# The order of one DMA queue in a mixture-of-experts loop, and a fourth staging buffer in two slots

## The chip, the core and the metric

The kernel runs on one core of a Trainium2 chip. The time is the device time of one execution in microseconds, the median of three runs. Its engines are PE (TensorE), ACT (ScalarE), DVE (VectorE), POOL (GpSimd) and SP (SyncE), which here only issues DMAs.

## The reference, cut to what matters

Three layers follow each other: an attention over 2 x 8 heads of 768 rows, a mixture of eight experts in which each of 1536 tokens goes to one expert, and a feed-forward layer with a rational function in place of an activation.

```python
for e in range(E):                      # layer 2: N, D, E, F = 1536, 512, 8, 1024
    mask = expert_idx == e
    h = np.maximum(x[mask] @ w1[e], 0.0)
    out[mask] = gate_w[mask, None] * (h @ w2[e])
...
h = x @ w_in                            # layer 3: 512 -> 2048 -> 512
P = a[0] + a[1] * h + a[2] * h2 + a[3] * h3
Q = 1.0 + np.abs(b[0]) * np.abs(h) + np.abs(b[1]) * h2
return (g @ w_out).astype(np.float32)
```

`w_in` and `w_out` arrive as 64-bit floats, and the kernel has to turn them into 32-bit floats by bit operations.

## The kernel before

The tokens are sorted by expert and worked on in 17 **slots** of 128 rows (`NSL`, L1069; loop at L1075). Slot s does the first product of its rows (`gemm1(s)`, into `ph`), transposes the rows of slot s + 1 (`xtr`), does the second product of slot s - 1 (`gemm2(s - 1)`, into `py`) and transposes its own hidden rows (`htr(s)`, into `pht`, then `hhi` and `hlo`). This document counts a slot from its first matmul of `gemm1` (L901) to the next slot's.

Every product is done with operands split in a high and a low part. ACT writes the high part of a weight half (`whi`, L654) and DVE the low part (`wlo`, L657), from four raw buffers `rw[s % 2, part]` of 2 MB each. Neighbouring slots often have the same expert. Then neither the loads of `wload` (L533, with a condition) nor the split of `wsplit` take place; both are decided by a flag in a table that the program computes.

**The conversion jobs.** While the slots run, 26 jobs convert layer 3's weights, two to a slot in slots 1 to 11 (`job_at`, L1072), one to a slot in 12 to 15. Job j takes five steps. `conv_load` (L858) is issued one slot ahead: 512 KB into one of four buffers `cx` or, from job 22 on, into a part of `el`. `conv_a` (L862, ACT) writes the high words' absolute value into a buffer z of 256 KB, which is one of the eight parts of the tile `el`. `conv_c` (L867, POOL) clamps z, `conv_b` (L872, L875 and L878, DVE) shifts and joins the bits, and `conv_s` (L883) stores z to `wf` in the next slot. Jobs up to 17 take z = `el` part j % 6; later ones 4 + j % 3. Jobs 16 and 17 have parts 4 and 5, jobs 18 to 21 the parts 4, 5, 6 and 4. Parts 0 to 3 are the load buffers of jobs 22 to 25. Part 7 is used by no job; layer 3's first weights are loaded into it at L1002 from slot 14 on.

Nothing reorders the instructions: each engine takes them in the order in which the code writes them. On ACT a slot reads: high parts of the next first half, `relu`, `xhi`, the slot's `conv_a`, the scaling of `y` (L937), `hhi` (L919), high parts of the second half. So a `conv_a` that waits holds back `hhi`, without which the next `gemm2` can't begin. On SP a slot reads: the store of the sorted rows of `y` (`ysave`, L949), loads for layer 3, the next jobs' `conv_load`, `x2load` (L957), eight weight loads in two halves (`wload(s + 2, 0)` and `wload(s + 1, 1)`), and last `conv_s` of the slot before. `ysave` and each half of `wload` first read registers from the table.

Of the kernel before, what the change touches and what calls it, by code (L numbers as in the profile page):

```python
# [13 lines left out]
I32 = mybir.dt.int32  # L14
# [45 lines left out]
NX, NM = 22, 26  # L60
# [18 lines left out]
def tile_kernel(ctx, tc, I, out):  # L79
# [13 lines left out]
    el = elp.tile([P, 8, TT], F32, name="el")  # L93
# [429 lines left out]
    def wload(s, part, ks=range(4)):  # L523
        r = rw[s % 2, part]
        src = I["w1"] if part == 0 else I["w2"]
        if s > 1:
            ev = nc.sync.value_load(rg[0:1, 1, s:s + 1], min_val=0, max_val=E - 1)
            fl = nc.sync.value_load(rg[0:1, 3, s:s + 1], min_val=0, max_val=1)
        for k in ks:
            if s < 2:  # L530
                nc.sync.dma_start(out=r[:, k], in_=src[s, :, k])
            else:
                nc.sync.dma_start(out=r[:, k],  # L533
                                  in_=src[bass.ds(ev, 1), :, k].rearrange("o p f -> (o p) f"), cond=fl > 0)
# [81 lines left out]
    def gather(s):  # L616
        xg[s] = gx[s % 3]
        nc.gpsimd.indirect_dma_start(out=xg[s], out_offset=None, in_=xs,
                                     in_offset=bass.IndirectOffsetOnAxis(ap=idx[:, s:s + 1], axis=0))
# [207 lines left out]
    cv = []  # L827
# [4 lines left out]
    def wsplit(s, part, which="hl"):  # L832
        if s == 0:
            split(s, part)
        elif which != "hl":
            e = ENG.Activation if which == "h" else ENG.DVE
            fl = nc.values_load(rg[0:1, 3, s:s + 1], engines=[e], min_val=0, max_val=1)
            with tc.If(fl > 0):
                for k in range(4):
                    if which == "h":  # L840
                        shi(s, 4 * part + k)
                    else:
                        slo(s, 4 * part + k, nc.vector)
        else:
            fl = nc.values_load(rg[0:1, 3, s:s + 1], engines=[ENG.Activation, ENG.DVE], min_val=0, max_val=1)
            with tc.If(fl > 0):  # L846
                split(s, part)
# [4 lines left out]
    def conv_load(j):  # L852
        if cv:
            cvt[j] = cv[0].tile([P, 512, 2], I32, name="cvt")
        else:
            t = el[:, 2 * (j % 2):2 * (j % 2) + 2].rearrange("p a b -> p (a b)") if j >= NX else cx[j % 4]
            cvt[j] = t.bitcast(I32).rearrange("p (a b) -> p a b", b=2)
        nc.sync.dma_start(out=cvt[j].rearrange("p a b -> p (a b)"), in_=I["wio"][j // 2, :, j % 2].bitcast(I32))  # L858

    def conv_a(j):  # L860
        z = el[:, 6 + j % 2 if cv else j % 6 if j < NX - 4 else 4 + j % 3].bitcast(I32)
        nc.scalar.activation(out=z.bitcast(F32), in_=cvt[j].bitcast(F32)[:, :, 1], func=AF.Abs)  # L862
        cvt[j] = (cvt[j], z)

    def conv_c(j, eng):
        z = cvt[j][1].bitcast(F32)
        eng.tensor_scalar(out=z, in0=z, scalar1=CLO, scalar2=CHI, op0=ALU.max, op1=ALU.min)  # L867
# [14 lines left out]
    def conv_s(j):  # L882
        nc.sync.dma_start(out=wf[j // 2, :, j % 2], in_=cvt.pop(j).bitcast(F32))  # L883
# [9 lines left out]
    def gemm1(s):  # L893
        hi, lo = xTm.pop(s)
        ph = [ps_h.tile([P, 512], F32, name=f"ph{n}") for n in range(2)]
        for rl in (False, True):
            kn = [(k, n) for k in range(4) for n in range(2)]
            for k, n in kn:
                w = (wlo if rl else whi)[:, k, 512 * n:512 * n + 512]
                for l in (hi,) if rl else (hi, lo):  # L900
                    nc.tensor.matmul(out=ph[n], lhsT=l[:, k], rhs=w, start=(k == 0 and not rl and l is hi),  # L901
                                     stop=(k == 3 and rl))
        hsb[s] = (hb, ph)

    def relu(s):
        h, ph = hsb[s]
        for n in range(2):
            nc.scalar.activation(out=h[:, 4 * n:4 * n + 4], in_=ph[n].rearrange("p (a b) -> p a b", a=4),
                                 func=AF.Relu)
# [36 lines left out]
    def ysave(s):  # L946
        y = yt.pop(s)
        yv = nc.sync.value_load(rg[0:1, 2, s:s + 1], min_val=0, max_val=(MAXS - 1) * P)
        ins = nc.sync.dma_start(out=ys[bass.ds(yv, P)], in_=y).ins  # L949
        for c, l in xld.items():  # L950
            if s >= c + MAXS - NT + 1:
                tc.declare_no_dep(ins, l, reason=APART)
        ysv[s] = ins

    def x2load(c):
        xid[c] = xa.tile([P, DR], F32, name="x2", bufs=2)
        ins = nc.sync.dma_start(out=xid[c], in_=ys[c * P:(c + 1) * P]).ins  # L957
        for s, l in ysv.items():
            if s >= c + MAXS - NT + 1:
                tc.declare_no_dep(ins, l, reason=APART)  # L960
        xld[c] = ins
# [32 lines left out]
    def fload(c, p):  # L994
        if (c, p) in floaded:
            return
        if (c, p) in ((0, 0), (1, 0)):
            wr[c, p] = el[:, 7]
        else:
            wr[c, p] = ring[(len(floaded) - 2) % len(ring)]  # L1000
        floaded.append((c, p))
        nc.sync.dma_start(out=wr[c, p], in_=wf[c, :, p])  # L1002

    def fsplit(c, p):
        if (c, p) in fdone:
            return
        fdone.append((c, p))
        r = wr[c, p]
        hi, lo = fsp[c % FH][p]
        nc.scalar.activation(out=hi, in_=r, func=AF.Copy)  # L1010
        (nc.gpsimd if cv else nc.vector).tensor_tensor(out=lo, in0=r, in1=hi.bitcast(F32), op=ALU.subtract)  # L1011
# [51 lines left out]
    def regather(s):  # L1063
        nc.gpsimd.indirect_dma_start(out=xg[s], out_offset=None, in_=xs,
                                     in_offset=bass.IndirectOffsetOnAxis(ap=idx[:, s:s + 1], axis=0))
# [3 lines left out]
    NSL = MAXS - 2  # L1069
    cxp = cx_.enter_context(tc.tile_pool(name="cx", bufs=1, reuse_waits="tile"))  # L1070
    cx += [cxp.tile([P, 1024], F32, name=f"cx{i}") for i in range(4)]
    job_at = {s: (2 * s - 2, 2 * s - 1) for s in range(1, NX // 2 + 1)}  # L1072
    for j in range(NX, NM):
        job_at[j - NX // 2 + 1] = (j,)
    for s in range(NSL + 1):  # L1075
        mine = job_at.get(s, ())
        if s == NX // 2 + 1:
            cx_.close()
            xb = ctx.enter_context(tc.tile_pool(name="xb", bufs=1, reuse_waits="tile"))
            x2.append((xb.tile([P, 4, TT], F32R, name="x2h0"), xb.tile([P, 4, TT], F32R, name="x2l0")))  # L1080
        if s and s + 2 < NSL:
            gather(s + 2)
        if s > 1:
            ysave(s - 2)
        if s >= NSL - 2:
            fsplit(s - (NSL - 2), 0)
        if s >= NSL - 3:
            fload(s - (NSL - 3), 0)
        for j in job_at.get(s + 1, ()):
            conv_load(j)  # L1090
        if 0 <= s - (NSL - 6) < 6:
            x2load(s - (NSL - 6))
        if s < NSL:
            gemm1(s)
            if STOP and s == 1:
                moe.close()
                rawr.close()
                return
            if s + 2 < NSL:
                wload(s + 2, 0)  # L1100
            if s + 1 < NSL:
                wload(s + 1, 1)
            for j in job_at.get(s - 1, ()):
                conv_s(j)
            if s + 1 < NSL:
                wsplit(s + 1, 0, "h")
            relu(s)
            if s + 1 < NSL:
                xtr(s + 1)
                wsplit(s + 1, 0, "l")  # L1110
            if s == 0:
                regather(1)
                for i in range(2):
                    nc.gpsimd.tensor_copy(out=gts[:, i:i + 1], in_=xg.pop(i)[:, DM:DM + 1])
            for j in mine:
                conv_a(j)
            for j in mine:
                conv_c(j, nc.gpsimd)
        if s > 0:
            gemm2(s - 1)  # L1120
            if s == NSL - 1:
                wsplit(s, 1, "h")
                htr(s)
            if s == NSL:
                elem_a(0)
                elem_b(0)
                elem_c(0)
            gemm2e(s - 1)
            if s == NSL - 1:
                wsplit(s, 1, "l")  # L1130
                fg1(0)
            if 0 <= s - (NSL - 5) < 4:
                x2prep(s - (NSL - 5))
        if s < NSL - 1:
            htr(s)
            wsplit(s, 1)
        for j in mine:
            for k in range(3):
                conv_b(j, k)
# [102 lines left out]
    for i in range(NI + 2):  # L1242
        j = conv_at.get(i, 0)
# [32 lines left out]
        if i + 1 in conv_at:  # L1276
            conv_a(conv_at[i + 1])
# [100 lines left out]
```

## Time and profile before

| | |
|---|---|
| time, median of 3 runs | 634.88 us (634.71 to 638.09) |
| profiled execution | 635.7 us |
| its span, first to last instruction | 633.9 us |
| PE busy | 578.4 us (91%) |
| DVE, ACT, POOL busy | 478.5, 417.8, 289.3 us |
| mean granted TensorE clock | 0.969 of full speed |

The span has three parts: attention and sorting to about 109 us, the 17 slots to about 344 us, and layer 3. The times of rows are microseconds from the span's start. A slot can be read from PE's rows: two `gemm1` that follow each other begin a slot apart.

### The profile page before, as it was taken

The page shows a single profiled execution, that of the slowest core. Times are in us where ns is not written, and L with a number is a line of the kernel's source. Part 1 is how long each engine was busy: PE and PEld are TensorE (multiplying, and loading weights), DVE is VectorE, ACT ScalarE, POOL GpSimd, SP SyncE. Part 2 cuts the span into 40 slices and gives each one's busy share as a digit, 9 for nine tenths or more (in the row PEclk, how much of TensorE's full clock was granted, in tenths as well). Part 3 has the DMA queues.
Part 4 walks back from the last instruction along what each step waited for, and adds up shares of the span by engine and source line. Part 5 has one row for each costly group of instructions (what it writes and reads, how often), then busy time and mean ns, then how long its engine had stood idle before and what let it go on. Part 6 is the DMA issues. An engine that isn't in the chain of part 4 may idle for free. (4 is left out here: it accounts for less than half of the span.)

```text
span 633.9 us, 10217 instructions
## 1 busy us (share of the span) xinstructions
PE 578.4 (91%) x3112; PEld 468.2 (74%) x3112; DVE 478.5 (75%) x1012; ACT 417.8 (66%) x719; POOL 289.3 (46%) x313
## 2 busy tenths in 40 slices
PE   4888984999999998879999899989999999999994
PEld 4777973688888887668887677777777777888883
DVE  6978877787845893369767777888988867877874
ACT  6987644775535672276765888766767887776672
POOL 7948822537334540454131654424244664432324
PEclk9989985999999999979999999999999999999998
DMA  9999541587669984779873422211114200000101
GB/s 273 321 306 295 169 166 50 165 335 250 232 204 308 397 288 150 229 243 336 323 249 101 134 73 94 67 51 50 51 50 150 77 24 1 34 34 1 51 17 67
DMA packets 37854, 101.65 MB, mean 160 GB/s; under 512 B 5977, under 2 KB 6105, under 8 KB 37794
## 3 DMA queue, kind: packets, MB, share of 16 engines
q1 hardware_dynamic: 35314, 92.81, 44.6%
q0 software_dynamic: 2480, 8.15, 3.6%
q8 instruction: 25, 0.41, 0.3%
q14 instruction: 35, 0.29, 0.1%
HBM read 119.51 MB, written 19.18 MB: 219 GB/s over the span
## 5 line engine op out<-in xcount | busy, mean ns | idle before, releaser
L867 POOL TENSOR_SCALAR el<-el 128x512 f32<-128x512 f32 x32 | 68.2, 2139 | 111.4 <-ACT el L862 111.4
L1051 POOL TENSOR_TENSOR wlo<-el,whi 128x512 fp32r<-128x512 f32 (+1 forms) x33 | 43.1, 1306 | 84.6 <-issue 44.7
L657 DVE TENSOR_TENSOR wlo<-rw,whi 128x1024 fp32r<-128x1024 f32 x62 | 74.6, 1263 | 2.1 <-issue 1.4
L654 ACT ACTIVATE whi<-rw 128x1024 fp32r<-128x1024 f32 x64 | 63.2, 1053 | 9.7 <-POOL wlo L657 4.4
L930 PE MATMUL py<-whi,hhi 128*128 128x512 f32 x136 | 56.1, 412 | 8.6 <-ACTq L846 8.6
L887 PE MATMUL hg<-x2h,whi 128*128 128x512 f32 (+1 forms) x148 | 58.7, 396 | 3.2 <-DVE el L1045 3.2
L888 PE MATMUL hg<-x2h,wlo 128*128 128x512 f32 (+1 forms) x148 | 57.7, 390 | 0.0
L889 PE MATMUL hg<-x2l,whi 128*128 128x512 f32 (+1 forms) x148 | 57.5, 389 | 0.0
L901 PE MATMUL ph<-whi,xhi 128*128 128x512 f32 x136 | 56.4, 415 | 0.7 <-ACT xhi L647 0.7
L1043 DVE SCALAR_TENSOR_TENSOR el<-el,ab,hg 128x512 f32<-128x512 f32 (+1 forms) x49 | 36.0, 735 | 26.5 <-ACT hg L1039 26.1
L901 PE MATMUL ph<-whi,xlo 128*128 128x512 f32 x136 | 55.1, 405 | 0.2 <-issue 0.2
L920 DVE TENSOR_TENSOR hlo<-pht,hhi 128x512 fp32r<-128x512 f32 x34 | 21.8, 682 | 43.8 <-ACT hhi L919 31.3
L930 PE MATMUL py<-whi,hlo 128*128 128x512 f32 x136 | 54.7, 402 | 0.0
L889 PE MATMUL acc<-wlo,whi 128*128 128x512 f32 x130 | 51.7, 398 | 2.0 <-POOL wlo L1011 1.7
L1029 ACT ACTIVATE el<-hg,ab 128x512 f32<-128x512 f32 (+1 forms) x49 | 33.2, 677 | 30.6 <-PE hg L889 30.5
L887 PE MATMUL acc<-whi 128*128 128x512 f32 x130 | 51.3, 395 | 2.1 <-DVE part L1221 1.0
L888 PE MATMUL acc<-whi,wlo 128*128 128x512 f32 x130 | 51.2, 394 | 1.2 <-POOL wlo L1051 1.2
L1031 DVE SCALAR_TENSOR_TENSOR el<-el,ab,hg 128x512 f32<-128x512 f32 (+1 forms) x49 | 35.9, 732 | 18.1 <-ACT el L1030 18.1
L1037 ACT ACTIVATE el<-el 128x512 f32<-128x512 f32 (+1 forms) x49 | 30.6, 624 | 28.5 <-DVE el L1031 28.0
L1033 DVE SCALAR_TENSOR_TENSOR el<-el,ab,hg 128x512 f32<-128x512 f32 (+1 forms) x49 | 36.1, 737 | 1.7
L1030 ACT ACTIVATE el<-hg,ab 128x512 f32<-128x512 f32 (+1 forms) x49 | 37.4, 763 | 0.0
L930 PEld LDWEIGHTS py<-whi,hhi 128*128 128x128 f32 x136 | 26.2, 193 | 14.7 <-ACTq L846 9.1
(354 smaller groups left out, 1557.2 us busy)
## 6 DMA issues: line engine op xcount, KB each, us to landing
rw<-w SPq DMA_DIRECT2D x136, 512.0 KB
cx<-wio SPq DMA_DIRECT2D x22, 512.0 KB
wf<-el SPq DMA_DIRECT2D x32, 256.0 KB
vw<-vp SPq DMA_DIRECT2D x8, 585.0 KB
ys<-y SPq DMA_DIRECT2D x17, 257.0 KB
xg<-wf SPq DMA_DIRECT2D x13, 256.0 KB
xs<-xall SPq DMA_DIRECT2D x12, 257.0 KB
x<-ys SPq DMA_DIRECT2D x12, 257.0 KB
```

Of the source, the lines that this page charges most:

```text
L654: nc.scalar.activation(out=whi[:, i], in_=rw[s % 2, i // 4][:, i % 4], func=AF.Copy)
L657: eng.tensor_tensor(out=wlo[:, i], in0=rw[s % 2, i // 4][:, i % 4], in1=whi[:, i].bitcast(F32), op=ALU.subtract)
L867: eng.tensor_scalar(out=z, in0=z, scalar1=CLO, scalar2=CHI, op0=ALU.max, op1=ALU.min)
L887: nc.tensor.matmul(out=o, lhsT=lh, rhs=rh, start=start, stop=False)
L888: nc.tensor.matmul(out=o, lhsT=ll, rhs=rh, start=False, stop=False)
L889: nc.tensor.matmul(out=o, lhsT=lh, rhs=rl, start=False, stop=stop)
L901: nc.tensor.matmul(out=ph[n], lhsT=l[:, k], rhs=w, start=(k == 0 and not rl and l is hi), stop=(k == 3 and rl))
L930: nc.tensor.matmul(out=py, lhsT=l[:, f], rhs=w, start=(f == 0 and not rl and l is hi), stop=(f == 7 and rl))
L1030: nc.scalar.activation(out=u, in_=h, func=AF.Identity, scale=ab[:, 3:4], bias=ab[:, 2:3])
L1033: nc.vector.scalar_tensor_tensor(out=u, in0=u, scalar=ab[:, 1:2], in1=h, op0=ALU.add, op1=ALU.mult)
L1043: nc.vector.scalar_tensor_tensor(out=u, in0=u, scalar=ab[:, 0:1], in1=h, op0=ALU.add, op1=ALU.mult)
L1051: nc.gpsimd.tensor_tensor(out=lo, in0=g, in1=hi.bitcast(F32), op=ALU.subtract)
```

## The change

On SP the slot's DMAs are put in another order: after `ysave` comes the first half of the weights (`wload(s + 2, 0)`), then `x2load`, the stores `conv_s` of the slot before, the loads `conv_load` of the slot after, and last the second half of the weights (`wload(s + 1, 1)`). And jobs 18 to 21 take the `el` parts 4, 5, 6 and 7 instead of 4, 5, 6 and 4.

```diff
     def conv_a(j):
-        z = el[:, 6 + j % 2 if cv else j % 6 if j < NX - 4 else 4 + j % 3].bitcast(I32)
+        z = el[:, 6 + j % 2 if cv else j % 6 if j < NX - 4 else j - NX + 8 if j < NX else 4 + j % 3].bitcast(I32)
...
-        for j in job_at.get(s + 1, ()):
-            conv_load(j)
-        if 0 <= s - (NSL - 6) < 6:
-            x2load(s - (NSL - 6))
         if s < NSL:
             gemm1(s)
...
             if s + 2 < NSL:
                 wload(s + 2, 0)
+            if s >= NSL - 6:
+                x2load(s - (NSL - 6))
+            for j in job_at.get(s - 1, ()):
+                conv_s(j)
+            for j in job_at.get(s + 1, ()):
+                conv_load(j)
             if s + 1 < NSL:
                 wload(s + 1, 1)
-            for j in job_at.get(s - 1, ()):
-                conv_s(j)
```

The first place is SP's queue in slot 10, before the change: `ys` is the store of sorted rows, `cx0` and `cx1` are the loads of jobs 20 and 21, `rw00` and `rw11` the two halves of the weights (each load stands four times in the queue, here once), and the `wf` row is the stores of jobs 16 and 17.

```order
L949 DMA ys_1758<-y0_1750 128x514
L858 DMA cx0_1769<-wio 128x1024
L858 DMA cx1_1770<-wio 128x1024
L527 TENSOR_LOAD rg_160
...
L533 DMA rw00_68<-w1 128x1024
...
L533 DMA rw11_1740<-w2 128x1024
...
L883 DMA wf_1759<-el_64 128x512 x2
```

The same slot of the same queue after the change:

```order
L949 DMA ys_1758<-y0_1750 128x514
L527 TENSOR_LOAD rg_160
...
L533 DMA rw00_68<-w1 128x1024
...
L883 DMA wf_1759<-el_64 128x512 x2
L858 DMA cx0_1769<-wio 128x1024
L858 DMA cx1_1770<-wio 128x1024
...
L533 DMA rw11_1740<-w2 128x1024
```

The two stores have moved ahead of the two loads and of four weight loads, and the first half of the weights ahead of the two loads.

The second place is ACT's queue in slot 11, before the change, from `xhi` to the first `hhi`; the two L862 rows are `conv_a` of jobs 20 and 21, and the names in brackets are the counters that a row waits for (DMAHW3 to 5 count DMAs).

```order
L647 ACTIVATE xhi_1591<-px__3942 128x512 [waits DVE_49,PE_49]
L862 ACTIVATE el_64<-cx0_1769 128x512 [waits DMAHW4_49]
L838 UNCONDITIONAL_BRANCH
L862 ACTIVATE el_64<-cx1_1770 128x512 [waits DMAHW5_49,DMAHW3_49,DVE_49]
L937 ACTIVATE y0_1750<-py_3969,gts_1382 128x512 [waits PE_49]
```

The same rows after the change:

```order
L647 ACTIVATE xhi_1591<-px__3942 128x512 [waits DVE_49,PE_49]
L862 ACTIVATE el_64<-cx0_1769 128x512 [waits DMAHW2_49]
L862 ACTIVATE el_64<-cx1_1770 128x512 [waits DMAHW3_49]
L838 UNCONDITIONAL_BRANCH
L937 ACTIVATE y0_1750<-py_3969,gts_1382 128x512 [waits PE_49]
```

`conv_a` of job 21 waited for two DMAs and for DVE; now it waits for one DMA, its own load, as that of job 20 did and does.

## Rows read from the trace of the kernel before

**Rows 1.** Stretches: us; busy PE, PEld, DVE, ACT, POOL; PE clock; DMA share; GB/s.

```profile
208.09:220.63 12.54, 12.54 (x64) 10.25 (x62) 9.87 (x14) 8.25 (x14) 5.99 (x5) 1.00 1.03 409
233.15:245.67 12.52, 12.52 (x64) 10.24 (x62) 10.03 (x14) 6.50 (x10) 1.05 (x1) 1.00 0.67 208
245.67:261.37 15.70, 12.80 (x63) 10.31 (x62) 5.83 (x10) 5.00 (x9) 7.71 (x5) 1.00 0.36 103
261.37:281.95 20.58, 14.90 (x68) 11.98 (x66) 7.28 (x12) 9.15 (x14) 4.96 (x4) 0.83 0.77 257
281.95:294.91 12.96, 12.96 (x67) 10.67 (x66) 11.76 (x15) 8.00 (x13) 4.75 (x5) 1.00 1.01 401
294.91:307.89 12.98, 12.98 (x68) 10.69 (x66) 9.20 (x13) 8.16 (x13) 9.15 (x7) 1.00 0.90 291
```

**Rows 2.** PE in time: start, length, line, tiles, idle before and releaser.

```profile
251.38 0.60 PE L645 MATMUL px__3942<-cst,xg 128*128 128x128 f32 x4
254.87 0.50 PE L930 MATMUL py<-whi,hhi 128*128 128x512 f32 x1 [2.90 <-ACTq L846]
...
273.35 0.79 PE L930 MATMUL py<-whi,hhi 128*128 128x512 f32 x1 [5.68 <-ACTq L846]
273.94 0.63 PE L930 MATMUL py<-whi,hlo 128*128 128x512 f32 x1
...
277.23 0.39 PE L930 MATMUL py<-whi,hlo 128*128 128x512 f32 x1
```

**Rows 3.** ACT in time, slots 10 and 11, with rows of slots 8 and 13.

```profile
215.94 1.23 ACT L862 ACTIVATE el<-cx 128x512 f32<-128x512 f32 x2
...
239.85 0.60 ACT L647 ACTIVATE xhi<-px__3745 128x512 fp32r<-128x512 f32 x1
251.90 1.33 ACT L862 ACTIVATE el<-cx 128x512 f32<-128x512 f32 x2 [11.44 <-issue]
...
257.45 0.68 ACT L862 ACTIVATE el<-cx 128x512 f32<-128x512 f32 x1
271.04 0.66 ACT L862 ACTIVATE el<-cx 128x512 f32<-128x512 f32 x1 [12.90 <-issue]
...
293.38 0.69 ACT L862 ACTIVATE el<-el 128x512 f32<-128x512 f32 x1 [4.07 <-DMA wf<-el]
```

**Rows 4.** SP in time: issues of DMAs, how many in a row.

```profile
199.88 1.77 SPq L858 DMA_DIRECT2D cx<-wio  x2
...
234.02 4.75 SPq L533 DMA_DIRECT2D rw<-w  x8
238.82 0.81 SPq L883 DMA_DIRECT2D wf<-el  x2
240.75 0.34 SPq L949 DMA_DIRECT2D ys<-y  x1
241.70 2.13 SPq L858 DMA_DIRECT2D cx<-wio  x2
245.33 4.39 SPq L533 DMA_DIRECT2D rw<-w  x8
249.76 0.81 SPq L883 DMA_DIRECT2D wf<-el  x2
...
266.55 1.59 SPq L883 DMA_DIRECT2D wf<-el  x2
283.74 0.85 SPq L883 DMA_DIRECT2D wf<-el  x2
```

**Rows 5.** DVE in time: the last steps of jobs 15, 16 and 17.

```profile
231.18 0.98 DVE L878 SCALAR_TENSOR_TENSOR el<-cx,el 128x512 int32<-128x512 int32 x1
240.98 0.69 DVE L878 SCALAR_TENSOR_TENSOR el<-cx,el 128x512 int32<-128x512 int32 x1
242.77 0.69 DVE L878 SCALAR_TENSOR_TENSOR el<-cx,el 128x512 int32<-128x512 int32 x1
```

**Rows 6.** A shorter stretch in slot 11, columns as in rows 1.

```profile
247.00:257.00 10.00, 7.10 (x33) 5.60 (x32) 2.46 (x5) 3.87 (x8) 4.32 (x3) 1.00 0.14 53
```

## The prediction, written before the run

> **What bounds the kernel now.** I read the page's busy shares first (PE 91%), then the stretches slot by slot, then PE, ACT, SP and DVE in order of time around the two slots that stick out.
>
> In the slots PE is the bound: slots 8 and 10 take 12.54 and 12.52 us and PE is busy in all of it, and slots 13 and 14, which also transpose rows for layer 3, take 12.96 and 12.98, again full [rows 1]. Slot 11 takes 15.70 and slot 12 takes 20.58 [rows 1]. Slot 12 has the same extra transposes as slot 13, so the two are 15.70 - 12.52 = 3.18 and 20.58 - 12.96 = 7.62 us too long, 10.80 together.
>
> PE shows where: its first `gemm2` matmul stood idle 2.90 us in slot 11 and 5.68 us in slot 12 [rows 2]. These are 8.58 of the 10.80. After the longer gap the clock is down: the matmuls take 0.63 instead of 0.39 us for a while, and slot 12's mean granted clock is 0.83 where the others have 1.00 [rows 1, 2]. That costs about 1.7 us: 277.23 - 273.35 = 3.88 us for nine matmuls that take nine steps of about 0.235 us at full clock, 2.1. The rest is the restart.
>
> The releaser named is a branch in ACT's queue, so I look at ACT. In slot 10 its pair of `conv_a` (jobs 18 and 19) began at 251.90 after 11.44 us of idleness; in slot 11 `conv_a` of job 20 ran at once at 257.45, and that of job 21 only at 271.04, after 12.90 us [rows 3]. "Issue" says that the view sees no releaser among the engines. SP has it: the stores of jobs 16 and 17 were issued at 249.76, and 2.14 us later the pair starts; the stores of jobs 18 and 19 were issued at 266.55, and 4.49 us later job 21 starts [rows 4, 3]. Jobs 18 and 19 write `el` parts 4 and 5, which jobs 16 and 17 left there until they are stored, and job 21 writes part 4, which holds job 18. The stores stand last in SP's slot, behind the loads and eight weight loads. PE waits for `hhi`, which is behind `conv_a` on ACT.
>
> **The buffers.** Job 21 now writes part 7, job 20 part 6 as before. The order of ACT's waits shows for both only their own load. Nothing else holds part 7 in slot 11, since layer 3's load into it comes from slot 14 on. So the 12.90 us wait goes, and slot 12 falls to slot 13's 12.96: **-7.62**. What is late next is the load of the pair. It was issued at 241.70; now it stands behind the two stores and, as worked out below, is issued at about 244, some 9 us before ACT reaches it. ACT reached `xhi` 6.70 us into slot 10 (239.85 - 233.15) [rows 1, 3], so 245.67 + 7.3 = 253.0 in slot 11. The bound on the other side: if another wait kept job 21 at its place, this term is 0.
>
> **The stores.** Jobs 18 and 19 still write parts 4 and 5, so in slot 10 only the order can help. Job 16 is ready for storing at 240.98 + 0.69 = 241.67 and job 17 at 243.46 [rows 5]. Does SP get there? In slot 9 it can't pass before job 15 is done, at 231.18 + 0.98 = 232.16 [rows 5]. Then come one store issue (0.40), two loads (about 0.9), the second half of the weights, `ysave` and the first half. Eight weight loads with one read of registers inside take 4.75 us, and a read takes about 1.5 us (243.83 to 245.33) [rows 4]; four loads are then 1.6 and a half with its read 3.1. `ysave` ends 1.46 us after the stores before it (239.63 to 241.09) [rows 4]. 232.16 + 0.40 + 0.9 + 3.1 + 1.46 + 3.1 = 241.1: in time. With 2.14 us from issue to release, job 19 may start at 243.46 + 2.14 = 245.6 instead of about 252.6 (251.90 and half of 1.33). From there to PE's first matmul it took 254.87 - 252.57 = 2.30 us, so `gemm2` may begin at 247.9; PE itself comes to it at about 251.38 + 0.35 = 251.73 [rows 2]. That is 3.8 us of slack, and the 2.90 us stall goes too: **-3.18**.
>
> The uncertain size is the time from the store's issue to its release. The trace has 2.14, 4.49 and, for a store behind eight weight loads, 283.74 to 293.38 = 9.64 us [rows 3, 4]. By 4.49 job 19 starts at 248.0 and there is still no stall. By 9.64 it starts at 253.1, PE at 255.4, 3.7 us late: 0.5 us worse than now. The store now stands behind four weight loads. But in that stretch they move little: 208 GB/s in slot 10 and 53 GB/s from 247 to 257, against 409 in slot 8 [rows 1, 6], so few of the weight loads there can take place. So I take 2.14, the nearest row, and keep +0.5 as the other end.
>
> The Trainium skill speaks against this (DMA: Bandwidth & Descriptors, section on queues, rings and completion order): on each DMA engine the descriptors are consumed in the order of the ring, so what is put behind 2 MB of weights waits for them. The 9.64 us row agrees. Were those 2 MB moved in slot 10, at slot 8's 409 GB/s they would add 5.1 us, job 19 would start at 250.7 and PE at 253.0; the stall would be 1.3 instead of 2.90 us and the sum 1.3 us smaller.
>
> **What it costs.** No instruction is added: SP issues the same DMAs. Loads of conversions now stand behind the first half and two stores: (2.1 + 0.5) MB at 409 GB/s [rows 1], 6.4 us, in slots where the expert changes. The cover is the distance from issue to use: 199.88 to 215.94 for the jobs of slot 8, 16.1 us [rows 3, 4]. A landing after 6.4 + 2.6 (their own 1.05 MB) + 2.1 = 11 us is in time; once the cover is gone, each further microsecond beyond the 3.8 of slack costs PE one. The second half now waits for the stores, and so for `conv_b`; but before, both halves stood behind `conv_load`, which waits for the same `conv_b` (its buffer `cx` is the one that `conv_b` reads). The weights are needed a slot later, and PE never waited for them in rows 1's full slots. I cost all this at nothing, with 0 to 1 us as its bounds. The first half gets earlier, which gains nothing for the same reason.
>
> **The sum.** 7.62 + 3.18 = 10.80 off the profiled execution's 635.7: 624.9, and a span of 623.1. The median is 0.82 below the profiled execution, so 624.1. I expect the whole saving to reach the end, since layer 3 starts from the last slots and has no work of its own that runs on a clock of its own.
>
> **Rivals.**
> *Only the buffer helps.* Slot 11's stall stays, because SP arrives late or the stores are slow to be released. For it: the order of the queue gives slot 10 a margin of only half a microsecond on SP (241.1 against 241.67), though the slack is 3.8 behind it. Then 634.88 - 7.62 = 627.3, or 627.8 with the 0.5. Chance 0.11.
> *Given back in the next slots.* The two stalls let DVE and the DMAs catch up: over slots 11 to 14 they moved 103 x 15.70 + 257 x 20.58 + 401 x 12.96 + 291 x 12.98, 15.9 MB in 62.2 us, and must do so in 51.4 us: 309 GB/s, under slot 8's 409; DVE has 34.1 us of work in them [rows 1]. So the sums fit, but a second half queued behind 6.4 us of other transfers could stall slot 13 or 14 by as much: 624.1 + 6.4 = 630.5. Chance 0.07.
> *Slower: the conversion loads come late.* Where first halves are moved, `conv_load` lands after them, `conv_a` waits, and the stall of slot 11 shows up in other slots. It decides once a load takes over 16.1 + 3.8 = 19.9 us from issue to landing. With 3.18 us in each of six slots (about the number in which a first half of a new expert is loaded) it costs 19.1: 624.1 + 19.1 = 643. Against it: 11 us by the rates. Chance 0.04.
> *The change does nothing:* job 21 would have to wait for something in part 7. The list of its waits excludes it; I give it no share.
>
> **How the numbers follow.** The forecast has 0.78; its own range is 622.5 to 626.5 (a microsecond of cost, and the spread of the runs, which went up to 3.4 us). With the first rival's 627.3 to 627.8 and a part of the second, 622.0 to 629.0 holds 8 in 10 or a little more. About 0.5%, 3.2 us, is what a measurement can tell from no change here; faster means under 631.7. The forecast and the first rival lie there, and most of the second: 0.78 + 0.11 + 0.03 = 0.92, which I round down to 0.90 for what I haven't thought of; same 0.06; slower 0.04.
>
> **What would show it.** Right: slots 11 and 12 of 12.5 and 13.0 us, no idle time before `gemm2` in either, clock 1.00 in slot 12, the store of job 16 issued at about 242 (9 us into slot 10), `conv_a` of slot 10 starting 10 to 13 us into the slot and that of slot 11 right behind `xhi`. Wrong: a `conv_a` that waits in another slot, a `whi` that waits for `rw`, or stalls at the start of layer 3 that were not there.

## The result, and the profile after

The changed kernel takes 631.71 us (median of 21 runs), the kernel before 637.41 us (21 runs too): 5.70 us less. These medians count every run, while the ratios, here and below, leave out a kernel's slow runs, those over 1.5% above its fastest (5 of these 21, one of the kernel before's 21, 3 of the 6 of e4 below). The ratio is 0.9887, 95% interval 0.9862 to 0.9913: 7.2 us faster (5.5 to 8.8). 10.80 was forecast, and the time is 2.7 us above the predicted range.

The execution that was profiled with this timing took 641.43 us, far above the median, so the rows here are from a second profile of the same kernel (e1_after, span 631.0 us); the first one is called the first profile below. Stretches of that kernel, with the columns of [rows 1]; the rows are slots 0, 1, 10, 11 and 12:

```profile
112.36:123.00 10.64, 10.14 (x36) 7.64 (x37) 7.00 (x7) 5.75 (x9) 6.33 (x4) 0.72 0.22 44
123.00:140.80 17.80, 14.35 (x63) 11.16 (x61) 11.79 (x13) 8.08 (x12) 8.35 (x9) 0.90 0.99 355
...
240.99:253.51 12.52, 12.52 (x64) 10.25 (x62) 10.03 (x14) 7.18 (x11) 2.06 (x4) 1.00 0.56 191
253.51:266.05 12.54, 12.54 (x64) 10.26 (x62) 5.58 (x10) 5.49 (x11) 8.56 (x8) 1.00 0.84 244
266.05:279.02 12.97, 12.97 (x68) 10.69 (x66) 10.40 (x14) 8.14 (x13) 4.67 (x4) 1.00 0.90 321
```

Slots 11 and 12 took 15.70 and 20.58 before [rows 1] and take 12.54 and 12.97 now: 10.77 us less, as forecast. But slot 1 is 17.80 us long, with PE busy for 14.35 of them and a clock of 0.90. The prediction uses no row of slots 0 and 1 of the kernel before; here they are, in the same view:

```profile
109.06:119.71 10.65, 9.60 (x37) 6.99 (x37) 7.00 (x7) 5.77 (x9) 6.19 (x4) 0.80 0.30 70
119.71:132.94 13.23, 13.01 (x62) 10.10 (x61) 12.12 (x13) 7.93 (x12) 9.04 (x7) 1.00 0.96 336
```

Slot 1 has lost 17.80 - 13.23 = 4.57 us. All other slots agree within 0.1 us, and layer 3, from the start of slot 16 to the end, takes 313.07 us before and 313.06 after. From the start of slot 0 to that of slot 16 it is 211.79 us before and 205.55 after, 6.24 less. The first profile agrees with 205.21 us for that stretch, and its slot 1 is long too:

```profile
132.07:149.48 17.41, 14.56 (x62) 11.35 (x61) 11.70 (x13) 8.09 (x12) 8.52 (x9) 0.90 0.97 355
```

PE in order of time, columns as in [rows 2]: first slot 1, then slots 11 and 12.

```profile
132.68 1.09 PE L645 MATMUL px__1981<-cst,xg 128*128 128x128 f32 x4 [3.23 <-DMA xg<-xs,idx]
...
133.99 0.63 PE L930 MATMUL py<-whi,hlo 128*128 128x512 f32 x1
...
259.21 0.60 PE L645 MATMUL px__3942<-cst,xg 128*128 128x128 f32 x4
259.57 0.48 PE L930 MATMUL py<-whi,hhi 128*128 128x512 f32 x1
...
271.75 0.60 PE L645 MATMUL px__4145<-cst,xg 128*128 128x128 f32 x4
272.10 0.48 PE L930 MATMUL py<-whi,hhi 128*128 128x512 f32 x1
```

The first `gemm2` matmul of slots 11 and 12 follows the transposes with no bracket, that is, with no idle time before it: the stalls of 2.90 and 5.68 us [rows 2] are gone. In slot 1 the transposes of `px` wait 3.23 us for a DMA into `xg`, the rows that POOL gathers for slot 2; then matmuls take 0.63 us for a while, as they did in slot 12 before [rows 2].

ACT, answering [rows 3], in slots 10 and 11, then SP, answering [rows 4], in slot 10:

```profile
247.69 0.61 ACT L647 ACTIVATE xhi<-px__3745 128x512 fp32r<-128x512 f32 x1
251.88 0.67 ACT L862 ACTIVATE el<-cx 128x512 f32<-128x512 f32 x1 [3.58 <-DVE el L878]
253.81 0.67 ACT L862 ACTIVATE el<-cx 128x512 f32<-128x512 f32 x1 [1.26 <-DMA wf<-el]
...
260.21 0.61 ACT L647 ACTIVATE xhi<-px__3942 128x512 fp32r<-128x512 f32 x1
260.69 1.24 ACT L862 ACTIVATE el<-cx 128x512 f32<-128x512 f32 x2
```

```profile
247.72 1.47 SPq L533 DMA_DIRECT2D rw<-w  x4
249.56 2.13 SPq L883 DMA_DIRECT2D wf<-el  x2
251.74 0.92 SPq L858 DMA_DIRECT2D cx<-wio  x2
254.22 1.49 SPq L533 DMA_DIRECT2D rw<-w  x4
```

The wait of 11.44 us ahead of slot 10's pair is 3.58 and 1.26, and that of 12.90 us ahead of job 21 is gone: its `conv_a` runs right behind job 20's, 0.48 us after `xhi` started. The stores were issued 8.6 us into slot 10 (predicted 9), and the pair started 10.9 and 12.8 us into it (predicted 245.6 - 233.15 = 12.45 for the second).

### The profile page after: what moved, and what is told of

Same layout as the page of the kernel before. It is cut to its first block, busy times and chain, and to the rows that moved or that the text cites. A ratio compares the mean times of both kernels' runs of the same rounds, so it can differ in the third digit from the quotient of the medians.

```text
span 639.7 us, 10251 instructions
## 1 busy us (share of the span) xinstructions
PE 589.9 (92%) x3112; PEld 478.5 (75%) x3112; DVE 476.4 (74%) x1012; ACT 417.7 (65%) x719; POOL 284.4 (44%) x313
## 5 line engine op out<-in xcount | busy, mean ns | idle before, releaser
L867 POOL TENSOR_SCALAR el<-el 128x512 f32<-128x512 f32 x32 | 65.1, 2042 | 103.5 <-ACT el L862 103.5
L1029 ACT ACTIVATE el<-hg,ab 128x512 f32<-128x512 f32 (+1 forms) x49 | 33.1, 676 | 30.9 <-PE hg L889 30.8
L937 ACT ACTIVATE y<-py,gts 128x512 f32<-128x512 f32 x17 | 11.7, 685 | 45.2 <-PE py L930 40.3
L280 ACT ACTIVATE at<-sm,nm 128x118 f32<-128x118 f32 x96 | 29.7, 381 | 14.5 <-DVE nm L272 14.4
```

## Experiments

The theory from these rows: the stalls went as forecast, and the new order made one of its own in slot 1, by putting the second half of slot 1's weights beside POOL's row gathers. Rivals: the conversion loads do it, not the weights; slot 1's length is a whim of an execution, and the missing gain lies elsewhere. Kernels that ran together share the runs of the kernel before on their chip, 11 each time: e1 to e4 a median of 641.27 us, e5 to e8 of 636.43, e9 to e11 of 636.25.

**e1_after**: the changed kernel again.

> The changed kernel as it is, for a second profile and more times. Theory A (the new order issues the weights of slots 0 and 1 while the row gathers are on their way, so that slot 2's rows come late): slots 11 and 12 of 12.5 and 13.0 us, slot 1 again about 17.4 us with PE idle some 2.6 us before the transposes of slot 2's rows, and 10.8 - 4.2 = 6.6 us under the kernel before. Rival B (slot 1's stall belongs to the one execution that was profiled): slot 1 of 13.2 us and some 10.8 us under the kernel before.

Measured 630.84 us (6 runs), ratio 0.9864 [0.9801, 0.9928]; rows above. POOL's queue in slots 0 and 1 of this kernel, then SP's (start, length, line, idle before and releaser):

```profile
122.17 0.95 POOL L618 DMA_INDIRECT xg<-xs,idx  x1 [0.30 <-issue]
...
133.88 0.57 POOL L1114 COPY gts<-xg 128x1 f32<-128x1 f32 x1 [6.30 <-DMA xg<-xs,idx]
```

```profile
119.71 1.49 SPq L533 DMA_DIRECT2D rw<-w  x4
121.31 0.83 SPq L858 DMA_DIRECT2D cx<-wio  x2
122.23 3.19 SPq L531 DMA_DIRECT2D rw<-w  x4
```

The same two queues in the kernel before:

```profile
119.02 0.95 POOL L618 DMA_INDIRECT xg<-xs,idx  x1 [0.30 <-issue]
```

```profile
117.13 0.81 SPq L858 DMA_DIRECT2D cx<-wio  x2
119.81 2.53 SPq L533 DMA_DIRECT2D rw<-w  x4
122.44 2.27 SPq L531 DMA_DIRECT2D rw<-w  x4
```

POOL issues three gathers there, 1.3 us apart; the middle one (L618) fetches slot 2's rows. It is issued at about the same point of slot 0 in both (119.02 - 109.06 = 9.96 us in, and 122.17 - 112.36 = 9.81). The second half of the weights (L531) comes 13.38 us into slot 0 before and 9.87 after: 3.42 us behind the gather before, 0.06 us behind it now. PE uses the rows 10.5 us after the gather's issue (132.68 - 122.17), and it waited for them; before it used them 7.0 us after the issue (119.02 to 126.00), without a wait. POOL, which copies a column of slot 1's rows (L1114), waits 6.30 us for the third gather too. PE at slot 2's transposes in the kernel before:

```profile
126.00 0.60 PE L645 MATMUL px__1981<-cst,xg 128*128 128x128 f32 x4
```

Why the second half comes so much earlier shows in SP's waits of the kernel before (total us, times, longest):

```profile
SPq L858 <- DMA xs<-xall: 2.7, 1, 2.7
```

The conversion loads stand first in the old slot 0 and wait there for a store into `xs` (L519), with the register reads and both halves of the weights behind them. In the new order the reads and the first half stand ahead of these loads. From the issue of that store to the second half it takes 8.51 us before (113.93 to 122.44) and 5.00 in e1 (117.23 to 122.23).

**e2_buffer_only** and **e3_order_only**: each half of the change alone.

```diff
 # e2_buffer_only: of the change only this
+        z = el[:, 6 + j % 2 if cv else j % 6 if j < NX - 4 else j - NX + 8 if j < NX else 4 + j % 3].bitcast(I32)
 # e3_order_only: the whole change without that line
```

> The old order with the new buffer rule (jobs 18 to 21 in parts 4 to 7). Theory A: slot 12 falls from 20.6 to 13.0 us, slot 11 keeps 15.7, slot 1 keeps 13.2: 7.6 us under the kernel before, and so about as fast as the whole change or 1 us faster. Rival C (the two stalls come from the order, the buffer matters little): 3 us or less under.

> The new order with the old buffer rule (job 21 in part 4, which job 18 holds). Theory A: slot 11 of 12.5 us; in slot 11 job 18 is ready about 5 to 6 us after the slot's start (DVE ends it at about 250.9) and its store lands some 4 us later, about 2 to 3 us after ACT wants the part, which the slack of 3.8 us covers: slot 12 near 13.0, at most 15; slot 1 of 17.4. So 4 to 6.6 us under the kernel before, close to the whole change. Rival C' (without the fourth buffer slot 12's stall stays): slot 12 of 20.6, slot 1 of 17.4, 1 us over the kernel before.

Measured: e2 632.39 us, ratio 0.9899 [0.984, 0.9957]; e3 631.07 us, 0.987 [0.981, 0.993]. Slots 11, 12 and 15 of e2, then slots 1, 11 and 12 of e3:

```profile
247.66:263.35 15.69, 12.79 (x63) 10.30 (x62) 5.83 (x10) 6.15 (x12) 8.52 (x6) 1.00 0.38 105
263.35:276.32 12.97, 12.97 (x67) 10.68 (x66) 5.75 (x11) 7.61 (x12) 2.42 (x4) 1.00 0.95 320
...
302.35:316.15 13.80, 13.48 (x67) 10.65 (x66) 9.15 (x14) 11.19 (x16) 0.75 (x3) 1.00 0.97 334
```

```profile
121.49:139.39 17.90, 14.65 (x63) 11.25 (x61) 11.71 (x13) 8.08 (x12) 8.35 (x9) 0.90 0.98 358
...
252.11:264.65 12.54, 12.54 (x63) 10.25 (x62) 5.59 (x10) 4.35 (x8) 6.31 (x5) 1.00 0.83 242
264.65:277.65 13.00, 13.00 (x67) 10.74 (x66) 5.57 (x10) 8.35 (x13) 3.21 (x4) 1.00 0.70 227
```

The buffer alone mends slot 12 and leaves slot 11 as it was; slot 1 is unharmed (13.23). It also lost 0.8 us in slot 15, where ACT's `whi` waits for weights; why there, I did not find out. The order alone mends both slots and harms slot 1. So the order carries the harm, and with it the fourth buffer is not needed in this execution: job 21 still waits for the store, but that now ends in time. The margin is small. From the stores' issue (261.17) to job 21 it took 7.24 us, where I expected some 4, and the first `hhi` ended at 270.14 us, 0.58 us before PE began `gemm2`. ACT in slot 12 of e3, and PE behind it:

```profile
268.41 0.68 ACT L862 ACTIVATE el<-cx 128x512 f32<-128x512 f32 x1 [8.44 <-DMA wf<-el]
```

```profile
270.72 0.50 PE L930 MATMUL py<-whi,hhi 128*128 128x512 f32 x1
```

**e4_slot0_old**: the change, with slot 0's old order, and **e5_slot0_only**: the kernel before, with the new order in slot 0 alone.

```diff
 # e4_slot0_old: the change, and ahead of wload(s + 2, 0)
+            if s == 0:
+                for j in job_at.get(1, ()):
+                    conv_load(j)
...
-            for j in job_at.get(s + 1, ()):
+            for j in job_at.get(s + 1, ()) if s else ():
                 conv_load(j)
 # e5_slot0_only: before, and between wload(s + 2, 0) and wload(s + 1, 1)
-        for j in job_at.get(s + 1, ()):
+        for j in job_at.get(s + 1, ()) if s else ():
             conv_load(j)
...
+            for j in job_at.get(1, ()) if s == 0 else ():
+                conv_load(j)
```

> The changed kernel with slot 0 alone in the old order (loads of conversions, first half, second half). Theory A (in slot 0 the weights' loads are issued about 3.6 us earlier against the gathers): slot 1 back to 13.2 us, the rest as in the change, 10.8 us under the kernel before and 4.2 under the change. Rival D (it is the order in slot 1, where the next first half now goes ahead of the loads of conversions): slot 1 stays at 17.4 us, and the time is the change's.

> The kernel before with slot 0 alone in the new order (first half, which is skipped there, loads of conversions, second half). Theory A (the earlier second half of slot 1's weights competes with the row gathers): slot 1 of 17.4 to 17.9 us instead of 13.2, slots 11 and 12 of 15.7 and 20.6 as before: some 4.4 us over the kernel before. Rival D (slot 1's loss needs the rest of the new order, say slot 1's own): slot 1 of 13.2 us, the time of before.

Measured: e4 629.38 us, ratio 0.9765 [0.967, 0.9861]; e5 641.75 us, one run, where the kernel before has 636.43. Slot 1 of e4, then slots 1 and 11 of e5:

```profile
118.38:131.62 13.24, 13.01 (x63) 10.12 (x61) 12.12 (x13) 7.95 (x12) 7.90 (x7) 1.00 0.97 364
```

```profile
120.09:138.24 18.15, 14.63 (x63) 11.28 (x61) 11.70 (x13) 8.09 (x12) 8.68 (x9) 0.91 0.99 355
...
250.96:268.22 17.26, 14.36 (x63) 11.45 (x62) 5.83 (x10) 5.01 (x9) 7.71 (x5) 0.90 0.45 131
```

The old order in slot 0 takes the harm away, and the new order in slot 0 alone makes all of it (18.15 - 13.23 = 4.92 us, in one execution). From slot 0 to slot 16, e4 takes 201.03 us, 10.76 less than before: the whole forecast saving. Slots 11 and 12 of e5 keep their stalls; with 17.26 and 19.77 us they are 37.03 together, 36.28 before.

**e6_loads_last**: the change, but in slot 0 the conversion loads stand behind the second half. **e7_hold**: the change, but a store of 4 bytes of slot 2's gathered rows stands ahead of slot 0's second half on SP, so that these weights can't start before the gather has landed.

```diff
 # e6_loads_last: in slot 0
-            for j in job_at.get(s + 1, ()):
+            for j in job_at.get(s + 1, ()) if s else ():
                 conv_load(j)
...
                 wload(s + 1, 1)
+            for j in job_at.get(1, ()) if s == 0 else ():
+                conv_load(j)
 # e7_hold: (hold is a one-element DRAM tile)
                 conv_load(j)
+            if s == 0:
+                nc.sync.dma_start(out=hold, in_=xg[2][0:1, 0:1])
...
                 wload(s + 1, 1)
```

> The changed kernel with slot 0's loads of conversions moved behind the second half of the weights. Theory A: the weights start still 0.9 us earlier against the gathers, slot 1 stays at 17 us or more. Rival E (the loads of conversions, which the change moved close to the gathers, are what delays them): slot 1 of about 13.2 to 14 us, as they now come behind 2 MB.

> The changed kernel with one 4-byte store of the rows of slot 2 put in SP's queue ahead of slot 0's second half, so that the weights are not issued until gather 2 has landed; nothing else moves. Theory A: gather 2 lands within 6 us of its issue, slot 1 of 13.2 us (at most 13.8), 4.4 us under the change. Rival F (the gather is slow whatever SP does, because it comes behind the two others on POOL's queue): slot 1 stays at 17.4 us or gets longer.

Measured, one run each: e6 626.45 us, e7 624.01 us. PE at slot 2's transposes in e6, then in e7, and SP's queue in e7:

```profile
127.31 0.63 PE L645 MATMUL px__1981<-cst,xg 128*128 128x128 f32 x4 [2.16 <-DMA xg<-xs,idx]
```

```profile
125.08 0.60 PE L645 MATMUL px__1983<-cst,xg 128*128 128x128 f32 x4
```

```profile
117.09 0.83 SPq L859 DMA_DIRECT2D cx<-wio  x2
124.48 0.28 SPq L1105 DMA_DIRECT2D hold<-xg  x1
124.86 1.77 SPq L531 DMA_DIRECT2D rw<-w  x4
```

In e7 the gather was issued at 118.13 and the weights at 124.86, behind the hold. With the weights held back and the conversion loads where the change puts them, the wait is gone and slot 1 takes 13.22 us: the 1 MB of conversion loads alone does no harm to it. The gathers took 6.3 us (below), a little over the 6 that I expected. The hold also delays what stands behind the weights on SP, first of all slot 1's own first half, so e7 alone does not part the two. But that first half follows the gather by 4.82 us in e1 (126.99 - 122.17) and by 5.59 in e5 (125.00 - 119.41), both with the harm, and by 5.91 in e4 (123.51 - 117.60), which has none; the second half follows it by 0.06 us in e1, is issued 0.09 ahead of it in e5 and 2.33 behind it in e4. So the weights of the second half are what the gather could not stand beside. e6 missed in part: I expected slot 1 to be as bad as in the change (17 us or more), and it was 15.47. With the loads behind the weights the gap is 2.16 instead of 3.23 us, and no lower clock follows. Whether the loads bear the difference is open, since e9_after below has nearly the same gap with them in front.

The time of those three gathers from issue to landing, in the view of DMA issues: the issue, its count and the median in us. The kernel before, then e7, then e1:

```profile
xg<-xs,idx POOLq DMA_INDIRECT x3, 4.8
```

```profile
xg<-xs,idx POOLq DMA_INDIRECT x3, 6.3
```

```profile
xg<-xs,idx POOLq DMA_INDIRECT x3, 10.4
```

The same view gives 5.1 in e2, 5.3 in e4, and 5.4, 5.5 and 5.2 in e8, e10 and e11 (below); 8.8 in e6, 9.1 in e9_after (below), 9.5 in the first profile, 10.0 in e3 and 10.3 in e5. Seven profiles have the second half issued behind the gathers and show 4.8 to 6.3 us; six have it beside or ahead of them and show 8.8 to 10.4. The Trainium skill (DMA: Bandwidth & Descriptors, section on queues, rings and completion order) says that each DMA engine takes turns, packet by packet, among the queue rows that have work for it, so a gather on POOL's queue shares the engines with weights on SP's. These rows agree: the gathers take 1.4 to 2.2 times as long, though they stand in a queue of their own. The turns themselves no run here shows.

**e8_rotate**: the kernel before with its old order, the parts of `el` in such a rotation that no job of slots 10 to 12 meets a part that is still to be stored.

```diff
-        z = el[:, 6 + j % 2 if cv else j % 6 if j < NX - 4 else 4 + j % 3].bitcast(I32)
+        z = el[:, 6 + j % 2 if cv else j % 6 if j < 16 else (4, 5, 6, 7, 4, 5, 6, 4, 5, 6)[j - 16]].bitcast(I32)
```

> The old order throughout, with jobs 16 to 25 going round parts 4, 5, 6, 7, 4, 5, 6, 4, 5, 6, so that no job of slots 10 and 11 takes a part that waits for its store. Theory A: slots 11 and 12 of 12.5 and 13.0, slot 1 of 13.2, and up to 1 us lost in slots 14 and 15 as with the buffer alone: 9.9 to 10.8 us under the kernel before, some 3 to 4 under the change. Rival G (the stalls need the order): slot 11 or 12 keeps 3 us or more of its excess.

Measured 625.09 us (6 runs), ratio 0.9811 [0.978, 0.9843]. Slots 11 and 12 of it, and its `conv_a` pairs on ACT:

```profile
245.46:257.98 12.52, 12.52 (x63) 10.24 (x62) 5.58 (x10) 4.34 (x10) 5.55 (x6) 1.00 0.70 211
257.98:270.95 12.97, 12.97 (x67) 10.68 (x66) 8.77 (x13) 8.36 (x13) 3.92 (x4) 1.00 0.97 326
```

```profile
240.10 1.26 ACT L862 ACTIVATE el<-cx 128x512 f32<-128x512 f32 x2
252.64 1.23 ACT L862 ACTIVATE el<-cx 128x512 f32<-128x512 f32 x2
```

No wait ahead of either pair, and slot 1 takes 13.23 us: buffers alone, in another rotation, give the whole saving (201.07 us from slot 0 to slot 16). The loss of up to 1 us in slots 14 and 15 that I allowed for did not come; they take 12.97 us each.

**e9_after, e10_slot0_old, e11_rotate**: the change, e4 and e8 side by side on one chip.

> The changed kernel once more, beside the next two on one chip. By the slots: 6.4 us under the kernel before.

> The changed kernel with slot 0 in the old order, again. By the slots 10.8 us under the kernel before, and 4.2 to 4.6 under the change on the same chip. If its first ratio was luck: no more under the change than 1 us.

> The old order with the rotated parts, again: as the one before it, 10.8 us under the kernel before, within 0.5 us of the change with slot 0 in the old order.

Measured: 630.82 us, 0.9884 [0.9831, 0.9938]; 626.60 us, 0.9843 [0.9786, 0.99]; 626.85 us, 0.9857 [0.9794, 0.9921]. Both repairs beat the change, by about 4 us in the medians, though their intervals overlap with its. Between the two repairs no difference shows. Slot 1 of e9, and the wait of PE for the gathered rows in it:

```profile
124.77:140.38 15.61, 13.07 (x62) 10.10 (x61) 11.71 (x13) 8.05 (x12) 7.07 (x7) 1.00 0.96 352
```

```profile
133.53 0.63 PE L645 MATMUL px__1981<-cst,xg 128*128 128x128 f32 x4 [2.31 <-DMA xg<-xs,idx]
```

So the same kernel loses 2.4 us in slot 1 in one execution, 4.2 in the first profile and 4.6 in e1, and e10 and e11 lose none (13.22 each). Why e9 loses less stays open. That harm of 2.4 to 4.6 us is the size of the repairs' lead.

## Why the prediction was wrong

- *The buffers, -7.62.* Right in size and mechanism: slot 12 takes 12.97 us, and e2 shows that the buffer alone does it. That the order alone would do it as well (e3) I had not seen. Beside the new order the buffer takes nothing off: slots 11 and 12 are 25.54 us together in e3 and 25.51 in the change. So the sum of 10.80 holds for these two slots, but not its split into two terms.
- *The stores, -3.18.* Right: SP got to them 8.6 us into slot 10, they were released in time, and slot 11 takes 12.54 us. The bound of +0.5 did not come. Few weights are moved there, as [rows 6] said: in e1 the DMA engines moved nothing from 247.7 to 249.5 us, while the first half was issued ahead of the stores. The sum by the Trainium skill's rule (DMA: Bandwidth & Descriptors, section on queues, rings and completion order), that what is put behind weights in a ring waits for them, would have left 1.3 us of stall; no such stall is in slot 11. The 2 MB that this sum supposes ahead of the stores were not moved, so slot 11 does not test the rule.
- *What it costs, 0 to 1 us.* This is the step that failed; it measured 2.4 to 4.6 us. I costed the moved loads by what waits for *them*, the weights' users and `conv_a`, and by getting later. In slot 0 there are no stores, and the second half gets 3.5 us earlier. The cost falls on a transfer that the diff does not touch: POOL's gather of slot 2's rows, on another queue, comes late beside 2 MB of weights, and PE waits for it (3.23 us in e1, 2.31 in e9). e4, e5 and e7 show it, by undoing the new order there, by making it alone and by holding the weights back. The prediction's rows are of slots 7 to 14; rows of slot 0, with its gathers close to the moved weights, are missing.
- *The rivals.* None of them was it. "Given back in the next slots" was near in size (630.5), with the wrong place and mechanism. No conversion load came late: slots 2 to 10 and 13 to 15 are as long as before.
- *The sum.* By the ratio 10.80 - 7.2 = 3.6 us of gain are missing (2.0 to 5.3), and slot 1 lost 2.4 to 4.6 us in the three profiles of the change, which is enough to account for them. The forecast of the median was 7.6 us low. Of these 5.1 are missing gain by the medians, and the other 2.5 are the kernel before itself, whose median is 637.41 us in these 21 runs against 634.88 in the three shown.

## What to carry to other kernels

Here a DMA that was moved cost time by what it then ran beside, on another queue: where an order is changed for the sake of one stage, go through the first and the last pass of the loop too, and look for small transfers on other queues (here a gather) with a user that is close behind. Where a wait is for a buffer, look for another rotation of the buffers before the order of a queue is changed: it moves no transfer out of its place by hand, and here e8's gave the whole saving with none of the harm, while e2's left one stall and lost 0.8 us in slot 15.

## Not expected of the hardware

- Three gathers of rows took 4.8 us (median) with 2 MB of weights issued 3.4 us behind the middle one (the kernel before), and 10.4 us with these beside it (e1).
- The clock after a gap on PE: the mean granted clock of slot 1 was 1.00 with 2.16 and 2.31 us of idleness (e6, e9), 0.90 with 2.62, 3.02 and 3.23 (the first profile, e3, e1) and 0.91 with 3.30 (e5). Beyond the gap, slot 1 lost 4.57 - 3.23 = 1.3 us in e1 and 15.61 - 13.23 - 2.31 = 0.1 us in e9. In slot 11 a gap of 2.90 us left 1.00 in the kernel before [rows 1, 2], while e5's slot 11, with a gap of 2.90 too, had 0.90: the length of the gap alone does not decide.
- The part ahead of slot 0 is the same program in all kernels, and yet slot 0 starts anywhere from 107.5 us (e11) to 121.4 us (the first profile), while layer 3 takes 313.1 to 314.5 us. In the three profiles of the changed kernel the start differs by up to 9.1 us, slots 0 to 15 by 2.1 and layer 3 by 1.4: most of what differs between these executions arises at the start.
